# An unused 384-byte tile ahead of wo: shifting where the operands of a two-stage kernel lie in SBUF

## The chip, the cores and the metric

The kernel runs on one NeuronCore of a Trainium2 chip. The metric is device time in microseconds (us). The profile names the engines PE (TensorE matmul), PEld (TensorE weight load), DVE (VectorE), ACT (ScalarE), POOL (GpSimd) and SP (SyncE, which issues most DMAs). On-chip memory (SBUF) has 128 partitions; an address below is a byte address within each partition, the same for all 128.

## The reference

Two stages, over 8 x 4160 = 33,280 tokens of 192 features. First a light convolution: each of 8 heads has 7 weights per token, softmaxed over the 7, which blend the token with its 6 predecessors. Then a maxout feed-forward layer with 768 hidden units.

```python
w = np.exp(weight_gen - np.max(weight_gen, axis=-1, keepdims=True))
w = w / (np.sum(w, axis=-1, keepdims=True) + 1e-09)
x_unf = x_pad[:, idx, :].reshape(B, S, K, H, group)      # 7 shifted copies
x = np.einsum('bshk,bskhg->bshg', w, x_unf).reshape(B * S, D)
h = np.maximum(np.maximum(x @ w1, x @ w2), x @ w3)       # 192 -> 768
out = h @ w_out                                          # 768 -> 192
```

## The kernel before

**Precision.** TensorE multiplies in the type float32r (4 bytes an element). To keep float32 accuracy, each operand is split into a high and a low part, and a product is made of several matmuls: `xa_hi`, `xa_lo` hold the parts of the first 128 features of the tokens, `xb` and `xc` the mixed parts of the last 64; `wa_hi`, `wa_lo`, `wb_hi`, `wb_lo` hold the parts of w1, w2, w3; `h_hi`, `h_lo` the parts of the hidden layer; `wo` the parts of w_out (192 high and 192 low columns side by side for each of 6 blocks j of 128 hidden units).

**Tiling.** The 260 tiles of 128 tokens go in 65 chunks of 512 tokens. For each chunk POOL multiplies the 7 shifted tokens by their weights (`product`, L246), DVE sums the 7 (`total`, L261), DVE and ACT transpose the result through a tile called `room` (`transpose`; the first three chunks use TensorE), and ACT and POOL split it into xa_hi, xa_lo, xb, xc (`parts`).

**The matmuls.** All of them are written at L329, in `product_of`. The array is used as two halves of 64 rows: each product is run once with partitions 0 to 63 and once with 64 to 127, as two independent streams which run side by side and add into the same PSUM tile `ph`. Two kinds of product feed it:

- *up* (`up`, `maximum`): the weights are the stationary operand (128 columns), and the tokens stream: xa_hi, xa_lo, xb or xc, 512 columns of 4 bytes, that is 2048 bytes of each partition. A chunk has 9 steps (3 pairs of j times 3 weight matrices) of 9 matmuls per half: 81 matmuls of 512 columns per half. A step begins and ends so that both halves meet in the same operands once a step.
- *down* (`down`): a slice of h_hi or h_lo (128 columns, 512 bytes) is the stationary operand, and wo streams: `wo[:, j]`, 384 columns (1536 bytes), against h_hi, then `wo[:, j, :192]` (768 bytes) against h_lo. A chunk has 4 token tiles times 6 j: 24 such pairs per half. For the last chunk j = 0 to 3 are run ahead of j = 4 and 5.

ACT copies the first of three up products to `m`, DVE takes the maximum with the second and third (L378), ACT and POOL split m into h_hi and h_lo (L381, L385); ACT and DVE add the two column halves of a down product (L410, L411). A table `OPENING` and some tuples written by hand set which step's work is issued at which tick; no address enters into this.

**Where the tiles lie.** Each pool's tiles lie one behind another in the order in which they are first asked for, and the pools one behind another: `const` first. In the built program (bytes from the partition's start, those of a tile with two buffers as "first, second"):

| tile | size of one | before | before, mod 2048 | before, mod 512 |
|---|---|---|---|---|
| ident | 512 | 16512 | 128 | 128 |
| wa_hi / wa_lo | 9216 | 17024 / 26240 | 640 / 1664 | 128 / 128 |
| wb_hi / wb_lo | 9216 / 4608 | 35456 / 44672 | 640 / 1664 | 128 / 128 |
| wo | 9216 | 49280 | 128 | 128 |
| xa_hi | 2048 | 124544, 126592 | 1664 | 128 |
| xa_lo | 2048 | 128640, 130688 | 1664 | 128 |
| xb | 2048 | 132736, 134784 | 1664 | 128 |
| xc | 2048 | 136832, 138880 | 1664 | 128 |
| h_hi | 12288 | 140928, 153216 | 1664 | 128 |
| h_lo | 12288 | 165504, 177792 | 1664 | 128 |
| m (four buffers) | 2048 | from 190080 | 1664 | 128 |

The six rows wo[:, j] begin 1536 bytes apart: at 128, 1664, 1152, 640, 128 and 1664 (mod 2048) for j = 0 to 5, each 128 mod 512. The slices of a weight tile begin a multiple of 512 bytes apart, as those of h_hi and h_lo do.

Of the kernel before, what the change touches and what calls it, by code (L numbers as in the profile page):

```python
# [13 lines left out]
F32 = mybir.dt.float32  # L14
# [7 lines left out]
P = 128  # L22
# [76 lines left out]
def lightconv_maxout_kernel(  # L99
# [55 lines left out]
    const = ctx.enter_context(tc.tile_pool(name="const", bufs=1))  # L155
# [10 lines left out]
    wa_lo = const.tile([P, NJ, 3, P], F32R, name="wa_lo")  # L166
    wb_hi = const.tile([P, NJ, 3, P], F32R, name="wb_hi")
    wb_lo = const.tile([P, NJ // 2, 3, P], F32R, name="wb_lo")
    wo = const.tile([P, NJ, 2 * D], F32R, name="wo")


# [533 lines left out]
```

## Time and profile before

| | |
|---|---|
| median of 3 runs | 1700.21 us (1697.39 to 1700.39) |
| the profiled execution | 1699.39 us |
| its span, first to last instruction | 1697.6 us |
| PE busy | 1657.2 us (98% of the span), 16794 matmuls |
| PEld busy | 1466.1 us (86%) |
| POOL / ACT / DVE busy | 1426.2 / 1145.8 / 1124.6 us (84% / 67% / 66%) |
| mean granted clock of TensorE | 0.998 |
| DMA | 79.51 MB, 47 GB/s on the mean |

The trace lists each matmul with its start and its duration. Matmuls are pipelined: one starts before the one ahead has left the array, so the durations overlap, and what a matmul costs is read from the distance between one start and the next in the same half (called its *pitch* below). In the timeline "64x512" is the streamed operand (64 partitions, 512 columns), "64*128" the part of the array that is used, and "x2" means that both halves start the same kind of matmul together.

### The profile page before, as it was taken

What the parts mean: (1) busy time and instruction counts of PE and PEld (TensorE: products, weight loads), DVE (VectorE), ACT (ScalarE), POOL (GpSimd) and SP (SyncE); (2) the same over time, 40 slices, a digit from 0 to 9 for tenths busy, and PEclk for the clock granted to TensorE, in tenths of its full rate; (3) what the DMA queues carried; (4) which work ended last, traced back from release to release, by engine and by line L of the source; (5) the groups of instructions that cost most, each with busy time, mean ns of one, the idle gap of its engine ahead of it and who ended that gap; (6) DMA issues with size and microseconds to landing.
All of it is one profiled execution on the core that took longest, in us unless ns stands there. A gap on an engine that the chain in (4) does not pass through costs nothing.

```text
span 1697.6 us, 42191 instructions
## 1 busy us (share of the span) xinstructions
PE 1657.2 (98%) x16794; PEld 1466.1 (86%) x16794; DVE 1124.6 (66%) x1552; ACT 1145.8 (67%) x2896; POOL 1426.2 (84%) x844
## 2 busy tenths in 40 slices
PE   3899999999999999999999999999999999999999
PEld 2598889889889889889988988988988988988998
DVE  7966766666666666666666666666666666666653
ACT  5657667667666766766766766766776776676672
POOL 6888888989888888888888888988888888888872
PEclk9999999999999999999999999999999999999999
DMA  7010101101010110101010110101011010101000
GB/s 236 1 70 10 70 29 52 70 20 60 20 70 15 66 70 21 60 21 70 11 70 21 60 70 20 61 20 70 11 70 61 27 63 20 70 11 46 20 11 29
DMA packets 20422, 79.51 MB, mean 47 GB/s; under 512 B 2320, under 2 KB 5128, under 8 KB 17536
## 3 DMA queue, kind: packets, MB, share of 16 engines
q1 hardware_dynamic: 20104, 76.54, 11.9%
q8 instruction: 131, 2.15, 0.5%
q14 instruction: 67, 0.55, 0.1%
q10 hardware_dynamic: 120, 0.28, 0.0%
HBM read 51.25 MB, written 25.56 MB: 45 GB/s over the span
## 4 chain that ended last, share of the span: by engine, by line
PE 94%; DVE 3%; ACT 1%; DMA 1%; POOL 1%; SPq 0%; issue 0%; DVEq 0%
PE ph L329 94%; DVE acc L261 1%; DVE m L378 0%; DMA wt<-in_weight_gen_dram 0%; DVE ph L483 0%; POOL r L246 0%; DVE ph L488 0%; DVE e L495 0%; DVE ph L481 0%; DVE ph L494 0%; DMA xt<-in_x_dram 0%; SPq L529 0%; ACT room L290 0%; SPq L521 0%; POOL h_lo L385 0%
## 5 line engine op out<-in xcount | busy, mean ns | idle before, releaser
L246 POOL TENSOR_TENSOR r<-xt,wt 128x1344 f32<-128x1344 f32 x260 | 721.4, 2814 | 0.6 <-DMA xt<-in_x_dram 0.4
L378 DVE TENSOR_TENSOR m<-ph,m 128x512 f32<-128x512 f32 x780 | 520.6, 685 | 197.4 <-PE ph L329 113.7
L329 PE MATMUL ph<-xa_hi,wa_hi 64*128 64x512 f32 x2340 | 630.8, 391 | 9.4 <-DVE m L378 3.1
L385 POOL TENSOR_TENSOR h_lo<-m,h_hi 128x512 fp32r<-128x512 f32 x390 | 503.3, 1301 | 161.7 <-ACT h_hi L381 157.0
L329 PE MATMUL ph<-xa_lo,wa_hi 64*128 64x512 f32 x2340 | 626.9, 388 | 1.0 <-DVE xa_lo L304 1.0
L329 PE MATMUL ph<-xa_hi,wa_lo 64*128 64x512 f32 x2340 | 626.1, 387 | 1.1 <-POOL wa_lo L498 1.1
L329 PE MATMUL ph<-xb,wb_hi 64*128 64x512 f32 x2340 | 626.0, 387 | 0.0
L329 PE MATMUL ph<-wo,h_hi 64*128 64x384 f32 x3120 | 595.5, 355 | 0.0
L329 PE MATMUL ph<-wo,h_lo 64*128 64x192 f32 x3120 | 522.3, 247 | 0.0
L381 ACT CAST h_hi<-m 128x512 fp32r<-128x512 f32 x390 | 241.8, 621 | 409.7 <-DVE m L378 406.6
L261 DVE TENSOR_REDUCE acc<-r 128x192 f32<-128x1344 f32 x260 | 401.8, 1547 | 125.5 <-POOL r L246 125.5
L290 ACT COPY room<-room 32x128 f32<-32x128 f32 x1488 | 440.8, 296 | 25.7 <-DVE room L284 7.5
L329 PE MATMUL ph<-xc,wb_lo 64*128 64x512 f32 x1170 | 453.1, 387 | 0.1
L329 PEld LDWEIGHTS ph<-wo,h_lo 64*128 64x128 f32 x3120 | 398.8, 188 | 2.5
L329 PEld LDWEIGHTS ph<-wo,h_hi 64*128 64x128 f32 x3120 | 398.4, 184 | 2.9 <-issue 0.4
L329 PEld LDWEIGHTS ph<-xa_hi,wa_hi 64*128 64x128 f32 x2340 | 338.7, 185 | 53.9 <-DVE m L378 3.9
L329 PEld LDWEIGHTS ph<-xa_hi,wa_lo 64*128 64x128 f32 x2340 | 338.4, 185 | 42.0 <-POOL wa_lo L498 1.5
L329 PEld LDWEIGHTS ph<-xa_lo,wa_hi 64*128 64x128 f32 x2340 | 338.7, 185 | 38.7 <-DVE xa_lo L304 1.5
L329 PEld LDWEIGHTS ph<-xb,wb_hi 64*128 64x128 f32 x2340 | 338.7, 185 | 38.4 <-ACT xb L308 0.3
L376 ACT COPY m<-ph 128x512 f32<-128x512 f32 x390 | 221.8, 586 | 38.5 <-PE ph L329 35.3
L411 DVE TENSOR_TENSOR o<-ph,ob 128x192 f32<-128x192 f32 x260 | 86.7, 353 | 234.5 <-ACT ob L410 234.5
L329 PEld LDWEIGHTS ph<-xc,wb_lo 64*128 64x128 f32 x1170 | 216.3, 185 | 20.9 <-POOL wb_lo L498 0.5
(54 smaller groups left out, 702.6 us busy)
## 6 DMA issues: line engine op xcount, KB each, us to landing
xt<-in_x_dram SPq DMA_DIRECT2D x20, 1728.0 KB, 7.1
out_dram<-o SPq DMA_DIRECT2D x64, 384.0 KB, 2.3
wt<-in_weight_gen_dram SPq DMA_DIRECT2D x21, 336.0 KB, 3.0
h_hi<-in_moe_w_dram SPq DMA_DIRECT2D x6, 256.0 KB, 4.8
xt<-in_x_dram SPq DMA_DIRECT2D x1, 1536.0 KB, 9.3
h_lo<-in_moe_w_dram SPq DMA_DIRECT2D x6, 192.0 KB, 4.8
room<-in_moe_w_out_dram SPq DMA_DIRECT2D x1, 1152.0 KB, 8.1
xt<-in_x_dram SPq DMA_DIRECT2D x1, 960.0 KB, 5.2
```

Source lines behind the costliest of these rows:

```text
L246: nc.gpsimd.tensor_tensor(r.rearrange("p (h g) k -> p k h g", g=G), xt[:, la + t : la + t + K].rearrange("p k (h g) -> p k h g", g=G), wt[ ...
L261: nc.vector.tensor_reduce(state["acc", c][:, t], r, axis=AX.X, op=ALU.add)
L290: pin(nc.scalar.copy(to[:, :, p : p + 32], blocks[p : p + 32, :, f : f + 32]))
L329: ins = nc.tensor.matmul(ph[:, :n], w[h], v[h], start=begins and half == 0 and q == 0, stop=ends and half == 1 and q == len(terms) - 1,)
L376: pin(nc.scalar.copy(m[:, :N], ph[:, :N]))
L378: pin(nc.vector.tensor_tensor(m[:, :N], ph[:, :N], m[:, :N], op=ALU.max))
L381: later(1, lambda: pin(nc.scalar.copy(hi, m[:, :N])))
L385: nc.gpsimd.tensor_tensor(lo, m[:, :N], hi.bitcast(F32), op=ALU.subtract)
L411: pin(nc.vector.tensor_tensor(o[:, t], po[:, :D], ob, op=ALU.add))
```

## The change

One tile more is asked for in the pool `const`, between wb_lo and wo. Nothing writes or reads it. It takes 96 x 4 = 384 bytes of each partition, so wo and every tile behind it begin 384 bytes later; the tiles ahead of it (ident, wa_hi, wa_lo, wb_hi, wb_lo) stay.

```diff
     wb_lo = const.tile([P, NJ // 2, 3, P], F32R, name="wb_lo")
+    const.tile([P, 96], F32, name="spacer")
     wo = const.tile([P, NJ, 2 * D], F32R, name="wo")
```

In the built program wo begins at 49664 (512 mod 2048, 0 mod 512), xa_hi at 124928 and 126976, xa_lo at 129024 and 131072, xb at 133120 and 135168, xc at 137216 and 139264 (all 0 mod 2048), h_hi, h_lo and m likewise at 0 mod 2048. The instructions of every engine, their operands' shapes and their order are the same in both programs.

## The prediction

> **What bounds the kernel now.** I read the page first, then the chain that ended last in order of time, then stretches of the timeline on PE. The page gives the engines' shares and the chain.
>
> ```profile
> PE 1657.2 (98%) x16794; PEld 1466.1 (86%) x16794; DVE 1124.6 (66%) x1552; ACT 1145.8 (67%) x2896; POOL 1426.2 (84%) x844
> PE ph L329 94%; DVE acc L261 1%; DVE m L378 0%; DMA wt<-in_weight_gen_dram 0%; DVE ph L483 0%; POOL r L246 0%; DVE ph L488 0%; DVE e L495 0%; DVE ph L481 0%; DVE ph L494 0%; DMA xt<-in_x_dram 0%; SPq L529 0%; ACT room L290 0%; SPq L521 0%; POOL h_lo L385 0%
> ```
>
> In the chain in order of time, one piece of 1524 us holds nothing but matmuls; in the table of windows the middle 1200 us are all PE.
>
> ```profile
> 170.18 1523.98 PE ph L329 x14710
> 400.00:1600.00 1200.00, 1200.00 (x12292) 1068.30 (x12290) 796.18 (x1065) 830.12 (x2117) 1041.31 (x603) 1.00 0.12 45
> ```
>
> So from 170 us on nothing is waited for, at full granted clock (the 1.00), and the time is the number of matmuls times their pitch. A chunk has 81 up matmuls and 24 down pairs per half, 2 x (81 + 48) = 258 in both; 12292 / 258 = 47.6 chunks in 1200 us, or 25.19 us a chunk, and 65 chunks make 1637 us. The rest of the span is the opening. POOL, the next busiest, works 1041 of the 1200 us, so PE could be 13% faster before POOL is the bound.
>
> The pitch of the up matmuls, from the timeline on PE: the xa_hi,wa_lo rows with x2 come back once in a step of 9 matmuls.
>
> ```profile
> 1002.39 0.39 PE L329 MATMUL ph<-xa_hi,wa_lo 64*128 64x512 f32 x2
> 1002.62 0.39 PE L329 MATMUL ph<-xa_hi,wa_hi 64*128 64x512 f32 x2
> 1002.85 0.39 PE L329 MATMUL ph<-xa_lo,wa_hi 64*128 64x512 f32 x2
> ...
> 1004.43 0.39 PE L329 MATMUL ph<-xa_hi,wa_lo 64*128 64x512 f32 x2
> ...
> 1012.60 0.39 PE L329 MATMUL ph<-xa_hi,wa_lo 64*128 64x512 f32 x2
> ```
>
> Five steps, 45 matmuls, take 10.21 us: 227 ns each. The same matmuls, at the same addresses, also ran once at half the clock, at 78 to 80 us (the 0.50 in the row of the windows):
>
> ```profile
> 78.00:80.00 2.00, 2.00 (x12) 1.54 (x12) 1.91 (x3) 0.47 (x2) 2.00 (x4) 0.50 0.00 0
> 78.26 0.63 PE L329 MATMUL ph<-xa_lo,wa_hi 64*128 64x512 f32 x2
> 78.68 0.63 PE L329 MATMUL ph<-xb,wb_hi 64*128 64x512 f32 x2
> ...
> 79.54 1.04 PE L329 MATMUL ph<-xa_hi,wa_hi 64*128 64x512 f32 x2
> 79.97 1.05 PE L329 MATMUL ph<-xa_lo,wa_hi 64*128 64x512 f32 x2
> ```
>
> From 78.26 to 79.97 four matmuls took 1.71 us, 427.5 ns each. Half of that is 213.75 ns: at full clock each up matmul is 13 ns longer than its array cycles account for. This excess of 6% is what a placement could give back, and the whole prediction turns on it.
>
> The down pairs, near the end where one half runs alone:
>
> ```profile
> 1688.09 0.36 PE L329 MATMUL ph<-wo,h_hi 64*128 64x384 f32 x1
> 1688.28 0.25 PE L329 MATMUL ph<-wo,h_lo 64*128 64x192 f32 x1
> 1688.37 0.36 PE L329 MATMUL ph<-wo,h_hi 64*128 64x384 f32 x1
> 1688.57 0.25 PE L329 MATMUL ph<-wo,h_lo 64*128 64x192 f32 x1
> 1688.66 0.36 PE L329 MATMUL ph<-wo,h_hi 64*128 64x384 f32 x1
> 1688.85 0.25 PE L329 MATMUL ph<-wo,h_lo 64*128 64x192 f32 x1
> 1688.94 0.35 PE L329 MATMUL ph<-wo,h_hi 64*128 64x384 f32 x1
> 1689.14 0.25 PE L329 MATMUL ph<-wo,h_lo 64*128 64x192 f32 x1
> 1689.22 0.36 PE L329 MATMUL ph<-wo,h_hi 64*128 64x384 f32 x1
> 1689.42 0.25 PE L329 MATMUL ph<-wo,h_lo 64*128 64x192 f32 x1
> 1689.51 0.35 PE L329 MATMUL ph<-wo,h_hi 64*128 64x384 f32 x1
> 1689.71 0.25 PE L329 MATMUL ph<-wo,h_lo 64*128 64x192 f32 x1
> 1689.79 0.45 PE L329 MATMUL ph<-wo,h_hi 64*128 64x384 f32 x2
> ```
>
> Six pairs take 1.70 us, 283 ns each, 197 for the 384 columns and 87 for the 192 on the mean. Together, 81 x 227 + 24 x 283 = 25.18 us a chunk, the 25.19 of the window.
>
> **The change, part by part.** The new tile itself is never touched and costs no instruction. Programs and orders are alike; only addresses differ, so there are as many matmuls, waits and DMAs as before. Four things move.
>
> *1. The streamed tokens, 1664 to 0 mod 2048.* 81 x 65 = 5265 up matmuls per half, all on the path that sets the end. Each now streams exactly one aligned block of 2048 bytes, and four of 512 where it touched five. What an aligned block is worth, no row shows: all that PE streams in an up matmul begins at 128 mod 512. From above the gain is bounded by the excess: 13 ns x 5265 = 68 us. From below nothing excludes a loss. I take zero, by the nearest row, which is the next one.
>
> *2. wo, 128 to 512 mod 2048.* Here the trace holds an experiment of its own. The rows wo[:, j] begin at 128, 1664, 1152, 640, 128 and 1664 mod 2048. A row of 1536 bytes that begins at 128 ends at 1664, inside one block of 2048; the other three starts run over the end of a block. In the thirteen rows above j runs from 0 to 3 for one token tile and begins again for the next, so all four starts are there, and the h_hi matmuls stand 0.28, 0.29, 0.28, 0.28, 0.29 and 0.28 us apart: the crossing of a 2048 boundary costs less than the 10 ns that the view resolves. Since x is moved for just this boundary, that row speaks for zero in part 1 too. It says nothing of 512, since all these starts are 128 mod 512. If the whole excess of a 384-column matmul went, at the up matmuls' rate 13 x 384 / 512 = 10 ns, 24 x 65 = 1560 pairs would give 15 us; I take zero.
>
> *3. The stationary slices of h, 128 to 0 mod 512.* These loads can matter, because the pair is partly set by them:
>
> ```profile
> 1688.29 0.18 PEld L329 LDWEIGHTS ph<-wo,h_hi 64*128 64x128 f32 x1
> 1688.39 0.19 PEld L329 LDWEIGHTS ph<-wo,h_lo 64*128 64x128 f32 x1
> 1688.57 0.18 PEld L329 LDWEIGHTS ph<-wo,h_hi 64*128 64x128 f32 x1
> ```
>
> The load for h_hi begins with the h_lo matmul (1688.28) and the next load begins 0.10 later, 20 ns after the h_hi matmul has started at 1688.37: the 87 ns of the h_lo matmul hide most of a load, not all, and the h_hi matmul stands for some 20 ns. If a load that doesn't straddle a 512 boundary were so much shorter that this stand went, 1560 x 20 ns = 31 us would come back; if each stand doubled, 31 us would be added. I take zero: load rows are 0.18 or 0.19 us, whatever slice they read.
>
> *4. All that the other engines and the DMAs write and read.* xt, r, acc, room, m, o and the rest move by 384 bytes with the tokens, so their places relative to each other stay. A few per cent on POOL, DVE or ACT would hide behind PE, which waits for none of them after 170 us; the cover is the 13% of POOL. In the opening, up to 78 us, PE does wait for them, but the changed addresses come with the same instructions on the same tiles.
>
> The sum is zero against the profiled execution's 1699.39 us, of which 1.8 lie outside the span. That execution is 0.8 us under the median of the runs, so I forecast the median, **1700.2 us**. A measurement of this kernel can tell some 0.2%, 3.4 us, from no change; that is 0.65 ns on each up matmul.
>
> Why the excess would not be one of placement: it isn't made of array cycles, since those would double at half clock (427.5 would then be 454). What remains is a limit on the rate at which 4-byte elements come from SBUF, 2048 bytes in 227 ns, which a start that is already a multiple of 128 bytes need not change. The 192-column row fits this: 87 ns for 768 bytes is the same rate, within 3%. The Trainium skill, "SBUF — State Buffer", section "Specifications (TRN2)", says SBUF is read by 16-byte lines and that a penalty falls on each step to a new line. By that rule the change does nothing, since 128 and 0 both begin a line; the trace agrees as far as it goes, the four starts of wo being alike.
>
> **The rivals.**
>
> *A. The whole excess is misalignment (faster).* For it: 13 ns is a stall that exists and is the same in every up matmul, and no aligned stream is in the trace to refute it. Against it: the wo rows, which show no price for the 2048 boundary. It gives 1700.2 - 68 = 1632 us, or 1617 with the 15 us of wo. The Trainium skill, "TensorE: Matmul & The Clock Gate", section "Wait — 56ns, not 53.3ns?", gives the warm pitch as columns over 2.4 GHz plus about 2.5 ns, 215.7 measured at 512 columns. The trace has 227 and disagrees; if alignment brought that pitch, an estimate from that page is 11 ns x 5265 = 58 us and 1642 us.
>
> *B. Each block of 512 bytes that is touched costs a part of the excess (faster).* Five blocks share 13 ns, 2.6 ns each; an aligned up matmul touches four and saves 2.6 x 5265 = 13.7 us. wo's 384 columns go from four blocks to three, another 2.6 x 1560 = 4.1 us. That gives 1682 to 1686 us. For it: 192 columns touch two blocks, and 87 ns is 7 more than their 213.75 x 192 / 512 = 80, between nothing and 13. Against it: a plain rate fits as well.
>
> *C. The streams now collide with the weight loads (slower).* Before, tokens and up weights both lay at 128 mod 512; now the tokens are at 0 and the weights stay at 128. Every up matmul runs beside the load for the next one. If SBUF serves the two reads from banks chosen by low address bits, a new distance could make them meet. Priced as a doubled excess, 13 ns x 5265 = 68 us, 1768 us; it decides from 0.65 ns on. In the down pairs both operands move together, so they would stay at 283 ns. Against it: the loads of the up weights begin at any of four places mod 2048, and the rows from 1002 on keep one pitch of 227.
>
> That the change does not do what it says is excluded: the built program has the new addresses.
>
> **How the numbers follow.** No change 0.57: the only crossing that the trace can price costs nothing, and the half-clock rows point to a rate. A 0.18: an unexplained excess of the right size, untested by any aligned row. B 0.12: it fits the three widths, and just as well as a rate does. C 0.13: no row for it, but no row with that distance either. So faster 0.30, same 0.57, slower 0.13. The likeliest case alone has 1696.8 to 1703.6 (0.2% to either side). The range adds A and B, down to A's 1632, and leaves C out: 1632 to 1704, with 0.87 less the part of A that goes on to wo.
>
> **What would show each step.** Right: after 170 us nine up matmuls still take 2.04 us and six down pairs 1.70, and 12292 matmuls stand in the window from 400 to 1600. A shows as nine in 1.92 to 1.94 us; B as nine in 2.02 us, and the pair under 281 ns; C as nine in over 2.05 us with an unchanged pair; part 3 as a pair down to some 263 ns with the up pitch unmoved. If the pitches stay and the time still moves, I am wrong about the opening, up to 78 us, or about the cover of POOL.

## The result, and the profile after

The changed kernel takes 1727.12 us (median of 4 runs, 1726.68 to 1727.89); the kernel before takes 1699.38 us in the same comparison. The ratio is 1.0165, with a 95% interval of 1.0148 to 1.0183: 28 us slower. The forecast of no change was wrong, and the time lies over the stated range (1632 to 1704).

The line numbers are one higher than before. The first rows are the page's busy times and the long piece of the chain in order of time; the third is the window of 400 to 1600 us, its first columns the busy time and the count of PE.

```profile
PE 1686.2 (98%) x16794; PEld 1499.9 (87%) x16794; DVE 1130.8 (66%) x1552; ACT 1148.4 (67%) x2896; POOL 1438.4 (83%) x844
```

```profile
149.90 1571.59 PE ph L330 x13982
```

```profile
400.00:1600.00 1200.00, 1200.00 (x12063) 1070.00 (x12061) 787.11 (x1045) 816.03 (x2075) 1030.45 (x593) 1.00 0.12 44
```

PE still waits for nothing after 150 us and the granted clock is still 1.00, but in the same 1200 us it gets through 12063 matmuls instead of 12292. That is 12063 / 258 = 46.76 chunks, 25.67 us each instead of 25.19. From 170 us on, when 60.5 chunks' worth of matmuls are left (1524 us at 25.19), 0.48 x 60.5 = 29 us; the spans differ by 27.3. So no wait was added and no other engine became the bound: the matmuls themselves got slower.

Which of them, the timeline on PE shows: first the up matmuls, one row a step, then six down pairs near the end.

```profile
1000.00 0.40 PE L330 MATMUL ph<-xa_hi,wa_hi 64*128 64x512 f32 x2
1000.24 0.40 PE L330 MATMUL ph<-xa_lo,wa_hi 64*128 64x512 f32 x2
...
1002.09 0.41 PE L330 MATMUL ph<-xa_hi,wa_hi 64*128 64x512 f32 x2
...
1004.18 0.41 PE L330 MATMUL ph<-xa_hi,wa_hi 64*128 64x512 f32 x2
```

```profile
1715.42 0.35 PE L330 MATMUL ph<-wo,h_hi 64*128 64x384 f32 x1
1715.62 0.25 PE L330 MATMUL ph<-wo,h_lo 64*128 64x192 f32 x1
1715.70 0.36 PE L330 MATMUL ph<-wo,h_hi 64*128 64x384 f32 x1
...
1717.13 0.45 PE L330 MATMUL ph<-wo,h_hi 64*128 64x384 f32 x2
```

Nine up matmuls take 2.09 us instead of 2.04, 232 ns each; six down pairs take 1.71 us, as before (1.70). Over the whole trace from 170 us on, the mean distance from the start of an up matmul to the next start in its half is 232.7 ns against 227.0; a pair takes 283.6 against 283.2. These means are called *pitch* and *pair* below. The trace doesn't name the half, so the records are assigned to the halves by their order and distance; another assignment gives the same pitches to 0.1 ns and the same pairs to 0.6 ns. 5265 x 5.7 ns = 30 us covers the loss.

### The profile page after: what moved, and what is told of

Its sections match the earlier page's. It is cut to its first block, busy times and chain, and to the rows that moved or that the text cites. A ratio compares the mean times of both kernels' runs of the same rounds, so it can differ in the third digit from the quotient of the medians.

```text
span 1724.9 us, 42191 instructions
## 1 busy us (share of the span) xinstructions
PE 1686.2 (98%) x16794; PEld 1499.9 (87%) x16794; DVE 1130.8 (66%) x1552; ACT 1148.4 (67%) x2896; POOL 1438.4 (83%) x844
## 4 chain that ended last, share of the span: by engine, by line
PE 96%; DVE 2%; DMA 1%; SPq 0%; issue 0%; POOL 0%; ACT 0%; ACTq 0%; DVEq 0%
PE ph L330 96%; DVE acc L262 1%; DVE m L379 0%; DMA wt<-in_weight_gen_dram 0%; DMA xt<-in_x_dram 0%; DVE ph L484 0%; DVE ph L489 0%; SPq L530 0%; DVE ph L482 0%; DVE e L496 0%; DVE ph L495 0%; SPq L522 0%; DVE red L216 0%; DVE xt L197 0%; POOL wt L218 0%
## 5 line engine op out<-in xcount | busy, mean ns | idle before, releaser
L247 POOL TENSOR_TENSOR r<-xt,wt 128x1344 f32<-128x1344 f32 x260 | 733.2, 2866 | 1.2 <-DMA xt<-in_x_dram 0.9
L330 PE MATMUL ph<-xa_hi,wa_hi 64*128 64x512 f32 x2340 | 637.2, 395 | 8.4 <-ACT xa_hi L301 2.8
L330 PE MATMUL ph<-xa_lo,wa_hi 64*128 64x512 f32 x2340 | 633.8, 392 | 1.0 <-DVE xa_lo L305 1.0
L330 PE MATMUL ph<-xa_hi,wa_lo 64*128 64x512 f32 x2340 | 633.1, 392 | 0.6 <-POOL wa_lo L499 0.6
L330 PE MATMUL ph<-wo,h_lo 64*128 64x192 f32 x3120 | 552.8, 247 | 0.0
L330 PE MATMUL ph<-xc,wb_lo 64*128 64x512 f32 x1170 | 458.5, 392 | 0.0
L330 PEld LDWEIGHTS ph<-wo,h_lo 64*128 64x128 f32 x3120 | 433.9, 188 | 0.1
L330 PEld LDWEIGHTS ph<-wo,h_hi 64*128 64x128 f32 x3120 | 429.5, 184 | 1.8 <-issue 0.4
L330 PEld LDWEIGHTS ph<-xa_lo,wa_hi 64*128 64x128 f32 x2340 | 343.3, 186 | 38.1 <-DVE xa_lo L305 1.5
L412 DVE TENSOR_TENSOR o<-ph,ob 128x192 f32<-128x192 f32 x260 | 86.8, 353 | 233.5 <-ACT ob L411 233.5
```

Of the source, the lines that this page charges most:

```text
L247: nc.gpsimd.tensor_tensor(r.rearrange("p (h g) k -> p k h g", g=G), xt[:, la + t : la + t + K].rearrange("p k (h g) -> p k h g", g=G), wt[ ...
L330: ins = nc.tensor.matmul(ph[:, :n], w[h], v[h], start=begins and half == 0 and q == 0, stop=ends and half == 1 and q == len(terms) - 1,)
L412: pin(nc.vector.tensor_tensor(o[:, t], po[:, :D], ob, op=ALU.add))
```

## The experiments

Theory D, formed on this result: an up matmul streams tokens while the weights for the next one are loaded, and its pitch depends on the distance between the addresses of the two, taken modulo some repeat. In the kernel before, tokens and up weights all begin at 128 mod 512; the change made the distance -128. The rivals: P, the pitch depends on where the streamed tokens begin; R, the loss comes from the other engines' tiles, which moved relative to the weights as well.

All the runs that leave nothing out, in one table; "distance" is the tokens' start minus the up weights' start, mod 256. Each ratio is taken to runs of the kernel before in the same comparison, whose medians were 1698.3 to 1699.4 us.

| run | distance | median us | ratio to before, 95% interval | pitch ns | pair ns |
|---|---|---|---|---|---|
| before | 0 | 1699.4 | | 227.0 | 283.2 |
| the change (gap 384) | 128 | 1727.1 | 1.0165 [1.0148, 1.0183] | 232.7 | 283.6 |
| e1_all_moved | 0 | 1697.9 | 0.9996 [0.9986, 1.0005] | 227.0 | 283.2 |
| e2_weights_only | 128 | 1727.5 | 1.0171 [1.0156, 1.0186] | 232.7 | 283.6 |
| e3_x_only | 128 | 1732.0 | 1.0197 [1.0181, 1.0212] | 233.6 | 283.3 |
| e4_h_only | 0 (wo minus h: 128) | 1703.7 | 1.0031 [1.0019, 1.0044] | 227.2 | 285.3 |
| e7_gap_16 | 16 | 1730.6 | 1.0186 [1.0170, 1.0201] | 233.5 | 283.4 |
| e5_gap_32 | 32 | 1731.2 | 1.0187 [1.0172, 1.0202] | 233.5 | 283.4 |
| e5_gap_64 | 64 | 1711.0 | 1.0067 [1.0052, 1.0082] | 229.3 | 283.4 |
| e7_gap_128 | 128 | 1726.6 | 1.0163 [1.0146, 1.0180] | 232.7 | 283.6 |
| e5_gap_192 | 192 | 1732.4 | 1.0195 [1.0180, 1.0210] | 233.6 | 283.6 |
| e5_gap_256 | 0 | 1698.1 | 0.9993 [0.9983, 1.0002] | 227.0 | 283.2 |
| e8_woven | 0 (low parts 252) | 1738.7 | 1.0234 [1.0219, 1.0250] | 234.8 | 283.6 |
| e8_woven_gap_128 | 128 (low parts 124) | 1721.8 | 1.0136 [1.0119, 1.0153] | 231.8 | 283.5 |

**Distance or place: which operands move**

```diff
 e1:
+    const.tile([P, 96], F32, name="ahead")
     ident = const.tile([P, P], F32, name="ident")
 e2: the same, and 32 elements (128 bytes) ahead of wo
+    const.tile([P, 32], F32, name="spacer")
     wo = const.tile([P, NJ, 2 * D], F32R, name="wo")
```

> The unused 384 bytes lie ahead of the whole pool const, so the up weights move too: tokens, weights, wo and h all begin at 0 mod 512, and every distance among them is that of the kernel before. Theory D (the pitch of an up matmul depends on the distance, mod 512, between the streamed tokens and the weights that are loaded beside it): 227 ns a matmul, nine in 2.04 us, 1699 us like the kernel before. Theory P (it depends on where the streamed tokens themselves begin, 0 being worse than 128 mod 512): 232 ns, nine in 2.09 us, 1727 us like the changed kernel.

> 384 bytes ahead of the pool const and 128 more ahead of wo: the up weights lie at 0 mod 512, all that follows them stays at 128 mod 512. D: the distance has changed (128 instead of 0), so the pitch rises over 227 ns, to some 232 if the sign of the distance does not matter: 1715 to 1735 us. P: the tokens begin where they did mod 512, so 227 ns and 1699 us.

The windows of 400 to 1600 us, e1 and then e2:

```profile
400.00:1600.00 1200.00, 1200.00 (x12302) 1068.26 (x12300) 795.71 (x1064) 831.26 (x2120) 1041.08 (x605) 1.00 0.12 44
```

```profile
400.00:1600.00 1200.00, 1200.00 (x12055) 1200.00 (x12053) 787.60 (x1047) 815.56 (x2074) 1031.62 (x592) 1.00 0.12 44
```

e1 puts tokens, wo and h at exactly the addresses of the changed kernel, and PE gets through 12302 matmuls, as before the change: P falls, since the tokens' own place is the same and the time is not. e2 leaves tokens, wo and h at their old places mod 512, moves the weights alone, and loses what the change lost (12055).

```diff
 e3:
     raw_down = xtp.tile([P, NJ * D * 2], F32, name="room", bufs=1).bitcast(U32)
+    xtp.tile([P, 96], F32, name="ahead_x", bufs=1)
...
         xc = xtp.tile([P, CH], F32R, name="xc")
+        if c == 0:
+            xtp.tile([P, 32], F32, name="behind_x", bufs=1)
 e4: only behind xc, with 96 elements (384 bytes)
```

> 384 bytes ahead of xa_hi and 128 behind xc: of all tiles only the tokens (xa_hi, xa_lo, xb, xc) are moved mod 512, to 0; weights, wo, h, m and the tiles of the other engines stay at 128. D and P alike: 232 ns an up matmul, 1727 us, down pairs 283 ns. Theory R (the loss comes from the other engines' tiles, which moved with the tokens relative to the weights): 227 ns and 1699 us.

> 384 bytes behind xc: of the operands of PE only h_hi and h_lo move, to 0 mod 512 (m and o move with them); tokens, up weights and wo stay at 128. The down matmuls get the distance that the up matmuls have in the changed kernel. D: the down pair rises over 283 ns, by 2 to 5 ns for the 384 columns and 0 to 2 for the 192, 3 to 11 us, unless the load of the weights hides it; the up pitch stays at 227. P: no change, 1699 us. R: the up pitch rises by what m and h, now at another distance from the tokens, cost.

The windows of 400 to 1600 us, e3 and then e4:

```profile
400.00:1600.00 1200.00, 1200.00 (x12018) 1048.24 (x12016) 783.95 (x1042) 812.26 (x2065) 1028.44 (x591) 1.00 0.12 44
```

```profile
400.00:1600.00 1200.00, 1200.00 (x12241) 1066.58 (x12239) 794.72 (x1060) 827.11 (x2108) 1040.30 (x602) 1.00 0.12 45
```

e3 moves the tokens alone and has the whole loss: R falls as its cause. It has 1 ns a matmul more than the change (5 us), at the same addresses of tokens and weights, so the rest is not quite without effect; no run took that apart. e4 is the same experiment for the down products: with h at 128 from wo, the pair rises by 2.1 ns (2.5 by the other assignment). 1560 x 2.1 ns = 3.3 us, and 0.2 ns on 5265 up matmuls 1.1 us; 5.4 us were measured, so up to 1 us of it is not accounted for. P had forecast no change. As D said, the rule isn't one of the tokens alone: it holds for both kinds of product in this kernel.

**The repeat: other gaps ahead of wo**

```diff
+    const.tile([P, 8], F32, name="spacer")     # 32 bytes; 16, 48 and 64 elements for 64, 192, 256
     wo = const.tile([P, NJ, 2 * D], F32R, name="wo")
```

> As the changed kernel, but the unused tile ahead of wo has 32 bytes: tokens and up weights stand 32 bytes apart mod 512 instead of 0; wo and h keep their distance. Theory D with banks that repeat after 512 bytes (D512): every distance but 0 gives other meetings of the two reads; which, no run has shown; 225 to 236 ns an up matmul, 1690 to 1745 us. D with a short repeat of 32 or 64 bytes: 32 is like 0, or its worst case. Theory A kept from the prediction (only whole blocks of 512 matter): 227 ns and 1699 us, since a tile that is moved by 32 from 128 touches as many blocks.

> The unused tile has 64 bytes. D512: another pitch than 227 ns, 225 to 236 and 1690 to 1745 us. D with a repeat of 64 bytes (or of 32) is out already, since 384 is 6 x 64 and is not like 0; so a pitch of 227 here would say that only some distances hurt.

> The unused tile has 192 bytes. D512: neither like 0 nor like 384. D with a repeat of 256 bytes (D256): 192 has no twin among the runs so far; 225 to 236 ns.

> The unused tile has 256 bytes. D256: 256 is like 0, so 227 ns, nine up matmuls in 2.04 us, 1699 us. D512: it is the farthest distance and has a pitch of its own, over 228 or under 226 ns.

Windows of e5_gap_192, then e5_gap_256:

```profile
400.00:1600.00 1200.00, 1200.00 (x12015) 1050.05 (x12014) 784.21 (x1042) 812.86 (x2065) 1046.31 (x592) 1.00 0.11 44
```

```profile
400.00:1600.00 1200.00, 1200.00 (x12294) 1066.80 (x12292) 795.63 (x1065) 832.09 (x2118) 1041.48 (x604) 1.00 0.12 45
```

A gap of 256 bytes does nothing that the runs can tell (12294 matmuls, before had 12292); each gap tried that is no multiple of 256 costs. With 32 bytes the pitch is 233.5 ns and with 64 bytes 229.3, so theory A as kept (227) is out. Two more gaps, 4 and 32 elements, went with the runs on one half:

> The unused tile ahead of wo has 16 bytes. D256 (the repeat is 256 bytes): 0 gives 227 ns, 32 gives 233.5, 64 gives 229; nothing says where 16 falls between 225 and 234; 1690 to 1732 us. Under 226 ns it would be faster than both kernels.

> The unused tile ahead of wo has 128 bytes. D256: 384 is 256 + 128, so this is the changed kernel over again: 232.5 ns an up matmul, 1727 us, though no streamed tile begins at a multiple of 512 or 2048. If what 384 costs has to do with whole multiples of 512 or 2048, then not 1727.

128 is the changed kernel over again, 12065 matmuls in the window against 12063, with no token tile at a multiple of 512 or 2048. So D256 holds in both pairs that test it (128 like 384, 256 like 0), whole blocks decide nothing, and 16 bytes are enough for the loss. No distance tried beats 0.

```profile
400.00:1600.00 1200.00, 1200.00 (x12065) 1070.04 (x12062) 787.26 (x1045) 816.47 (x2075) 1031.36 (x593) 1.00 0.12 44
```

**Inside a half, or between the halves**

```diff
             if half == 0:
                 state["ph", step, odd] = ps.tile([P, CH], F32, name="ph")
+            if half == 1:
+                terms = terms[-1:]
```

> The addresses of the kernel before. Left out: of the up products of partitions 64 to 127 all matmuls but the last of each group, so that for most of the time the half of partitions 0 to 63 streams alone. Read by its pitch, not by its time. If the 13 ns of excess come from the two halves sharing something, the pitch of a lone up matmul falls towards 214 ns. If they come from a half's own stream and its own weight load (theory D with the meeting inside a half, Dw), or from a plain rate, it stays at 227.

> The same cut, with the 384 bytes ahead of wo. Dw: a lone up matmul takes some 232.5 ns as in the changed kernel. If instead the stream of one half meets the weight load of the other half (Db), the loss goes with the neighbour: 227 ns.

Timeline on PE, the lone half's first matmul of each step of nine, at the old addresses and then with the 384 bytes:

```profile
1000.44 0.39 PE L329 MATMUL ph<-xa_hi,wa_hi 64*128 64x512 f32 x1
...
1002.48 0.39 PE L329 MATMUL ph<-xa_hi,wa_hi 64*128 64x512 f32 x1
...
1004.52 0.39 PE L329 MATMUL ph<-xa_hi,wa_hi 64*128 64x512 f32 x1
```

```profile
1009.77 0.39 PE L330 MATMUL ph<-xa_hi,wa_hi 64*128 64x512 f32 x1
...
1011.87 0.39 PE L330 MATMUL ph<-xa_hi,wa_hi 64*128 64x512 f32 x1
...
1013.96 0.39 PE L330 MATMUL ph<-xa_hi,wa_hi 64*128 64x512 f32 x1
```

Nine matmuls take 2.04 us and 2.09 to 2.10 us, just as with the neighbour. So what the stream meets is the load of its own half (Dw), and the 13 ns of excess at the good distance don't come from the other half either.

**What the 13 ns are: woven weights, short loads**

```diff
-    wa_hi = const.tile([P, NJ, 3, P], F32R, name="wa_hi")
-    wa_lo = const.tile([P, NJ, 3, P], F32R, name="wa_lo")
+    wa = const.tile([P, NJ, 3, P, 2], F32R, name="wa")
+    wa_hi, wa_lo = wa[:, :, :, :, 0], wa[:, :, :, :, 1]
...                                                    # wb_hi and wb_lo likewise
```

> The high and low parts of the up weights lie woven, element by element (hi, lo, hi, lo), so a load of 128 columns steps 8 bytes where it stepped 4 and walks 1024 bytes of SBUF where it walked 512; tokens still begin at the same residue of 256 as the weights. Nothing is left out. Theory D with meetings inside a half (Dw): while it loads, a load of twice the step keeps pace with the stream, if a load takes 128 column times of half the stream's rate; they then keep their distance, so they either meet all along or hardly at all; if the 13 ns of excess are made of such meetings, the pitch leaves 227 ns, up to 240 or down to 214. Theory Rate (the 13 ns are a plain limit of the rate of 4-byte elements): 227 ns or more, never less.

> Woven weights and 128 unused bytes ahead of wo, so stream and load start half a repeat apart. Dw: they keep pace half a repeat apart and don't meet: the pitch falls under 227, towards 214 ns, 1640 to 1690 us. If distance then decides nothing, as with the woven weights without a gap. Rate: at best 227 ns, 1699 us; if the meetings come back, 232 ns, 1727 us.

Loads in the window of 400 to 1600 us, of before and of e8_woven: count, busy us, mean ns of one.

```profile
L329 PEld LDWEIGHTS ph<-xa_lo,wa_hi 64*128 64x128 f32 x1716 | 247.7, 185 | 27.8
```

```profile
L330 PEld LDWEIGHTS ph<-xa_lo,wa 64*128 64x128 f32 x1680 | 254.1, 192 | 22.3
```

A woven load takes 192 ns instead of 185, and the order of the distances turns round: 0 is now worse (234.8) than 128 (231.8). So the way in which the load walks through SBUF matters, but keeping pace with the stream did not take the pitch under 227, as Dw had hoped. The woven low parts begin 4 bytes behind the high ones, so the distance is 0 or 128 for the high parts alone; what those 4 bytes cost, no run shows.

```diff
+            m = 80 if n == CH and 0 < q < len(terms) - 1 else P
             ins = nc.tensor.matmul(
-                ph[:, :n],
-                w[h],
+                ph[:m, :n],
+                w[h][:, :m],
```

> The addresses of the kernel before. Left out: the up matmuls between the first and the last of each group load 80 weight columns instead of 128, so hidden units 80 to 127 of each block miss those terms. An up matmul that is followed by a short one (xa_hi with wa_hi, xa_lo where... wb_hi is short, xb before xc) thus runs beside a load five eighths as long. If the 13 ns of excess are meetings of stream and load (theory M), those matmuls fall to some 222 ns, and the others, beside a full load, stay at 227; span some 15 us shorter. Theory Rate: 227 ns for all, the same span.

> The same short loads with the 384 bytes ahead of wo. Theory D: what the bad distance adds, 5.6 ns on the mean, comes from the load, so matmuls beside a short load lose some three eighths of it: 230.5 ns where a full load gives 232.6. With M as well, some 225.5. If the length of the load decides nothing, D is wrong about what it is that the stream meets.

At the good distance the mean pitch rose to 232.7 ns (1728 us): 233.4 beside a short load and 232.0 beside a full one. At the bad distance it fell to 230.5 (1718 us): 228.7 beside a short load and 232.8 beside a full one. D's part holds in its direction: at the bad distance a shorter load costs less. M's does not: at the good distance all matmuls got longer. A short load also makes the matmul that uses it one of 80 array columns ("64*80" in the timeline), so these runs don't part the one from the other. At the good distance the halves had also fallen out of step, so both were run with one half alone, which is e9's edit and e6's together:

> The addresses of the kernel before. Left out: of partitions 64 to 127 all up matmuls but the last of each group, and in the other half the weight columns 80 to 127 of the matmuls between the first and the last of a group. So a half streams mostly alone, beside loads of 128 and of 80 columns. With the neighbour there, short loads raised the pitch from 227 to 232 to 235 ns instead of lowering it. Rate: alone, beside a short load, 227 ns; the rise came from the neighbour, whose start had drifted away. Theory M (the 13 ns are meetings with the half's own load): under 225 ns beside a short load. If the pitch stays at 232 and more, the length of the load itself upsets the good distance.

> The same cut with the 384 bytes ahead of wo. D inside a half: alone, beside a full load, some 231 ns as in the run of one half with full loads; beside a short load 226 to 229, nearer to 227 by the three eighths of the load that are gone. If short and full loads give the same, the load isn't what the stream meets.

Timeline of the lone half with short loads, at the old addresses and then with the 384 bytes:

```profile
1010.34 0.39 PE L330 MATMUL ph<-xa_hi,wa_hi 64*128 64x512 f32 x1
...
1012.41 0.39 PE L330 MATMUL ph<-xa_hi,wa_hi 64*128 64x512 f32 x1
...
1014.49 0.39 PE L330 MATMUL ph<-xa_hi,wa_hi 64*128 64x512 f32 x1
```

```profile
1012.91 0.39 PE L331 MATMUL ph<-xa_hi,wa_hi 64*128 64x512 f32 x1
...
1014.99 0.39 PE L331 MATMUL ph<-xa_hi,wa_hi 64*128 64x512 f32 x1
...
1017.07 0.39 PE L331 MATMUL ph<-xa_hi,wa_hi 64*128 64x512 f32 x1
```

These rows have steps of 2.07 to 2.08 us in both; on the mean from 300 to 1600 us a step takes 2.08 us in both, against 2.05 and 2.09 with full loads in the runs before. So alone, a mix of short and full loads is 3.9 ns a matmul worse than full ones at the good distance (231.3 against 227.4) and 1.0 ns better at the bad one (231.4 against 232.4), and the distance hardly matters any more. At the bad distance a matmul beside a short load took 230.2 ns and one beside a full load 233.3: the direction is D's, the size not, since 226 to 229 and 231 were forecast. The good distance is thus good together with a load of 128 columns, 512 bytes or two whole repeats; whether the length in repeats is what counts was not tested. What the 13 ns are stays open: no run had a mean pitch under 227.0 ns, which fits a rate limit; the one test that could have shown the load in them (M) came out the other way, and it changed the phase of stream and load along with the length.

## Why the prediction was wrong

*Step 1, the streamed tokens.* This is the step that failed: "I take zero, by the nearest row, which is the next one." It measured +5.7 ns on 5265 matmuls. The row it leaned on, the four starts of wo, could not see the effect: wo's rows lie 1536 bytes apart and h's slices 512, so all pairs of stream and load had the same distance modulo 256, and a place modulo 2048 varied that decides nothing. What was taken for an experiment held the one quantity constant that mattered.

*Step 2 and step 3, wo and h.* Both zeros came out right (the pair went from 283.2 to 283.6), but not for the reasons given, and so by luck: stream and load moved together, as C had said of the down pairs. e4, which parts them, costs 2.1 ns a pair.

*Step 4, the other engines.* The cover held. POOL's product L247 went from 2814 to 2866 ns and the engine from 1426 to 1438 us of work, hidden under PE.

*The half-clock argument.* It showed that the excess is not made of array cycles; going on from there to "a limit on the rate" that placement need not touch was the gap in it. The changed kernel too ran at half clock for a while, with its distance of 128. First the row of the windows, with the granted clock of 0.50, then the timeline on PE:

```profile
56.40:59.60 3.20, 3.07 (x14) 2.68 (x16) 3.13 (x7) 3.18 (x8) 2.37 (x2) 0.50 0.01 3
57.98 1.02 PE L330 MATMUL ph<-xa_hi,wa_lo 64*128 64x512 f32 x2
58.41 1.02 PE L330 MATMUL ph<-xa_hi,wa_hi 64*128 64x512 f32 x2
58.84 1.01 PE L330 MATMUL ph<-xa_lo,wa_hi 64*128 64x512 f32 x2
59.26 0.82 PE L330 MATMUL ph<-xb,wb_hi 64*128 64x512 f32 x2
```

Three matmuls take 1.28 us, 427 ns each, as at the old distance (427.5). What the distance costs at full clock, 5.7 ns, is not there at half clock, so rows at half clock cannot tell whether a part of the time at full clock is one of placement. Against the sentence "a start that is already a multiple of 128 bytes need not change" stand three runs whose tokens begin at a multiple of 128: the change and e7_gap_128 with 5.7 ns and e3_x_only with 6.6. The rule on 16-byte lines, from the Trainium skill's "SBUF — State Buffer", "Specifications (TRN2)", did not help: 16 bytes, one whole line, cost 6.5 ns. And where the Trainium skill, "TensorE: Matmul & The Clock Gate", "Step-by-step: what each phase is for", says that loading the next weights doesn't steal SBUF read bandwidth from the running matmul, the runs differ: 2.04 or 2.09 us a step by the distance to that load alone.

*A and B* are out: with no unaligned block left (the change, e3) the pitch rose, and with the same aligned tokens and the old distance (e1) it was 227.0, neither A's 214 nor B's 224.

*C was the mechanism* as far as the runs show it: a stream slowed by its distance to the weight load beside it, in the up matmuls, with the down pairs untouched. The banks that C supposed behind it no run shows. Its price was mis-sized: 13 ns, taken from the excess for want of a row, where 5.7 were measured; 1768 us forecast for it, 1727 measured. The argument against it, that the up weights begin at four places mod 2048 and the pitch is the same beside each, has the flaw of step 1: those four places are one place modulo 256. With that seen, C had no row against it, 0.13 was too little, and a range that ended at 1704 left out the side on which the trace was blind.

## What to carry to other kernels

Before you move tiles, write down for each matmul the distance between the streamed operand and the weights that are loaded beside it, modulo 256. In this kernel, with its contiguous loads of 128 columns, all that kept it at 0 was free (256 bytes ahead of wo, 384 ahead of everything), and all that changed it cost 0.3 to 2%. Where the distance is 0 already, a padding tile between weights and activations should be a multiple of 256 bytes. For loads of another shape this has to be measured anew: with woven weights 0 was worse than 128, and with short loads it was no better. And before a row is used as evidence that something doesn't matter, check that the quantity in question varies in it.

## What the runs showed of the hardware that was not expected

- The pitch of an up matmul goes with the distance between its stream and the weights that are loaded beside it, and repeats after 256 bytes: 227.0 ns at 0 and 256, 233.5 at 16 and 32, 229.3 at 64, 232.7 at 128 and 384, 233.6 at 192. It isn't in proportion to the distance. The up loads themselves keep 184 to 185 ns each (before, and with gaps of 384 and 192 bytes); at half clock the pitch was 427 ns at distances of 0, 16, 128 and 192 alike.
- POOL's product, whose own tiles kept their distances, also went with the gap: 2814 ns on the mean before, 2866 with the change, 2954 with 192 bytes. e3_x_only, which moves no tile that this product reads or writes, has 2857, and e1_all_moved, which moves them to where the change has them, 2815: POOL's own addresses are not what it goes by. What it goes by is open; it was hidden under PE throughout. The group from the pages of e5_gap_192 and e3_x_only:

```profile
L247 POOL TENSOR_TENSOR r<-xt,wt 128x1344 f32<-128x1344 f32 x260 | 756.7, 2954 | 0.7 <-DMA xt<-in_x_dram 0.5
L246 POOL TENSOR_TENSOR r<-xt,wt 128x1344 f32<-128x1344 f32 x260 | 731.6, 2857 | 0.9 <-DMA xt<-in_x_dram 0.6
```
